# GpSimd waits by semaphore for the VectorE instructions at the shared SBUF port: attention and mixer on one core

## The chip, the cores and the metric

One core of a Trainium2 chip. The metric is device time in microseconds, the median of several runs. PE is TensorE, DVE VectorE, ACT ScalarE, POOL GpSimd, SP the engine that issues the transfers. DVE and POOL share a port to SBUF, the on-chip memory; the kernel's planner calls it `port`.

## The reference

Attention over 8 batches and 8 heads (sequence 576, head size 64) with a mask in blocks of 64, then a mixer over the sequence with a rank of 32 and a two-layer network, all in float32:

```python
scores = scale * np.matmul(q, k.transpose(0, 1, 3, 2))
scores = np.where(block_i >= block_j, scores, -1000000000.0)
attn = np.exp(scores - np.max(scores, axis=-1, keepdims=True))
attn = attn / (np.sum(attn, axis=-1, keepdims=True) + 1e-09)
x = np.matmul(attn, v)            # heads side by side: (8, 576, 512)
...
h = x.transpose(0, 2, 1) @ U @ V  # (576, 32), (32, 576)
u = x + h.transpose(0, 2, 1)
return u + np.maximum(u @ w_ch1, 0.0) @ w_ch2   # (512, 2048), (2048, 512)
```

## The kernel before, in words

**Precision.** A float32 operand goes through PE as a high part and a low part. ACT rounds the high part, and DVE or POOL subtracts it from the whole for the low part. So most products need three passes on PE, and each operand costs work on ACT and on DVE or POOL.

**Stages.** The program has two. Up to about 640 us the 64 heads run one after another: scores (L1224, L1228, L1229) into PSUM, row maxima on DVE (L1242), exponentials on ACT (L1253), the inverse of the row sums on DVE (L1269, L1270), the scaling of the probabilities `p` by it on POOL (L1279, five row tiles per head), transposes of `p` on PE (L1312), their halves on ACT and DVE (L1289, L1331), the product with v (L1371), the sum of its halves on DVE (L1379) and, after every second head, the mixing over the sequence (L1397 to L1444). From head 14 on, q and k are split too: ACT makes the high parts, POOL the low ones (L1170, L1171), and SP moves halves to the other partitions (L1173, L1174); POOL also makes the low half of v (L1193). Between these, PE works through the first part of the network (chunks of 288 tokens by 768 of the 2048 hidden columns: L651, L676), whose low halves of u POOL makes (L629, L635). The rest of the network, a block product in seven stages in the manner of Strassen (L897), fills the second part, from about 740 us to the end. Its sums and halves run on DVE and ACT (L822 to L858); POOL has nothing to do there.

**Weights.** They arrive as 64-bit words. `split64` (line 325) puts each piece together: ACT takes the absolute value of the upper word, POOL bounds it (L369), and DVE shifts it (L345), puts in the sign bit (L350) and the lower bits (L358). Low halves of scaled weights come from L466, those of batch 0's u from L620; for the block product POOL and DVE form sums and low halves 1280 columns wide (L753). `multiply` (L435) is a product of two columns, one number per partition.

**The order.** `Plan.add` (line 158) records each task with its engine, an assumed duration, a priority and what it reads and writes, and varies the duration by up to ±2% with a number drawn from `VARIANT`. `Plan.issue` (line 175) then walks through time: whenever an engine is free, it starts the ready task of the best priority, and the instructions are written down in that order, each engine's queue in its own. A task may be marked `port`; all POOL tasks count as marked. Line 201 doesn't start a marked task while another marked one runs:

```python
if all(b.pool for b in new) and not (port and tasks[n][7]):
    break
```

This shapes the order of the queues only. On the chip each engine goes through its queue on its own and waits by semaphore for the data that it needs, for nothing else. Marked on DVE are L345, L350, L358, L466, L620, L753, L824 and L834; not marked are `multiply` and the sums of the block product.

Of the kernel before, what the change touches and what calls it, by code (L numbers as in the profile page):

```python
# [27 lines left out]
T = 288  # L28
# [28 lines left out]

TAIL = {"PE": 165, "DVE": 78, "ACT": 105, "POOL": 20, "SP": 0}
INTO = {"PE": 355, "DVE": 60, "ACT": 60, "POOL": 200, "SP": 60}
NEAR, DL = 130, 3000  # L60
VARIANT = 11
START = {"DVE": 5750, "ACT": 2750, "POOL": 3300, "SP": 700}
COL = 0.4555
LA, MP = 900.0, 500.0
# [82 lines left out]
class Plan:  # L147
# [24 lines left out]
            b.users += 1  # L172
        self.tasks.append((engine, ns, prio, fn, deps, after, slots, port or engine == "POOL"))

    def issue(self):
        tasks = self.tasks
        users = [[] for _ in tasks]
        left = [len(t[4]) for t in tasks]
        for n, t in enumerate(tasks):
            for d in t[4]:  # L180
                users[d].append(n)
        others = [{tasks[u][0] for u in x} for x in users]
        ready = {e: [] for e in ENGINES}
        busy = dict.fromkeys(ready, False)
        port = False
        for n, t in enumerate(tasks):
            if not left[n]:
                heapq.heappush(ready[t[0]], (t[2], n))
        events, now, done = [], 0, 0
        for e, x in START.items():  # L190
            busy[e] = True
            heapq.heappush(events, (x, 0, -1, e))
        while done < len(tasks):
            for e, q in ready.items():
                if busy[e]:
                    continue
                later = []
                while q:
                    n = heapq.heappop(q)[1]
                    new = [b for b in tasks[n][6] if b.ap is None]  # L200
                    if all(b.pool for b in new) and not (port and tasks[n][7]):
                        break
                    later.append((tasks[n][2], n))
                    n = None
                else:
                    n = None
                for x in later:
                    heapq.heappush(q, x)
                if n is None:
                    continue  # L210
                for b in new:
                    b.ap = b.pool.pop(0)
                done += 1
                tasks[n][3]()
                busy[e] = True
                port = port or tasks[n][7]
                end = now + tasks[n][1]
                heapq.heappush(events, (end, 0, n))
                t = end + tasks[n][5] + TAIL[e]
                heapq.heappush(events, (t + 35, 1, n))  # L220
                for x in others[n]:
                    heapq.heappush(events, (t + INTO[x], 3 + ENGINES.index(x), n))
                if not tasks[n][5]:
                    heapq.heappush(events, (end + (0 if e == "PE" else NEAR), 2, n))
            now = events[0][0]
            while events and events[0][0] <= now:
                _, kind, n, *e = heapq.heappop(events)
                if e:
                    busy[e[0]] = False
                    continue  # L230
                if kind == 0:
                    busy[tasks[n][0]] = False
                    port = port and not tasks[n][7]
                    continue
                if kind == 1:
                    for b in tasks[n][6]:
                        b.users -= 1
                        if not b.users:
                            b.pool.append(b.ap)
                    continue  # L240
                for u in users[n]:

                    near = tasks[u][0] == tasks[n][0] and not tasks[n][5]
                    if kind == (2 if near else 3 + ENGINES.index(tasks[u][0])):
                        left[u] -= 1
                        if not left[u]:
                            heapq.heappush(ready[tasks[u][0]], (tasks[u][2], u))
# [6 lines left out]
def _dve(n):  # L254
    return 69 + 1.042 * n
# [13 lines left out]
def attention_then_mixer(  # L269
# [10 lines left out]
    nc = tc.nc  # L280
# [49 lines left out]
    def split64(fetches, shape, hi, lo, dst, prio, gate=(), part=slice(None), whole=None):  # L330

        n = 1
        for x in shape[1:]:
            n *= x
        rows = shape[0]
        st, zt = take(st_r, "st"), take(z_r, "z")
        s, z = st[:rows, :n, :], zt[:rows, :n]
        low, upp = s[:, :, 0], s[:, :, 1]

        def fetch():  # L340
            for f in fetches:
                f(s)

        def shift():
            nc.vector.tensor_scalar(  # L345
                out=z, in0=z, scalar1=3, scalar2=0x3FFFFFFF, op0=ALU.logical_shift_left, op1=ALU.bitwise_and
            )

        def put_upper():
            nc.vector.scalar_tensor_tensor(  # L350
                out=z, in0=upp, scalar=-(1 << 30), in1=z, op0=ALU.bitwise_and, op1=ALU.bitwise_or
            )

        def put_lower():
            o, l, x = z, low, z
            if whole:
                o, l, x = whole().bitcast(I32), *(a.rearrange("p (a b) -> p a b", a=2) for a in (low, z))
            nc.vector.scalar_tensor_tensor(  # L358
                out=o, in0=l, scalar=29, in1=x, op0=ALU.logical_shift_right, op1=ALU.bitwise_or
            )  # L360

        zf = f32(z)
        if len(shape) > 2:
            zf = zf.rearrange("p (a b) -> p a b", a=shape[1])
        add("SP", max(630 * len(fetches), 2.85 * n), prio, fetch, gate, [st], after=DL)
        add("ACT", _act(n, True) + (40 if n > 200 else 0), prio, lambda: nc.scalar.activation(f32(z), f32(upp), AF.Abs), [st], [zt])
        add(
            "POOL", 145 + 0.85 * n, prio,
            lambda: nc.gpsimd.tensor_scalar(out=f32(z), in0=f32(z), scalar1=MOST, scalar2=LEAST, op0=ALU.min, op1=ALU.max),  # L369
            [], [zt],  # L370
        )
        add("DVE", 50 + 0.55 * n, prio, shift, [st, zt], [zt], port=True)
        add("DVE", 13 + 1.15 * n, prio, put_upper, [st, zt], [zt], port=True)
        if whole:
            add("DVE", 100 + 1.15 * n, prio, put_lower, [st, zt], dst if isinstance(dst, list) else [dst], port=True)
            return
        add("DVE", 100 + 1.15 * n, prio, put_lower, [st, zt], [zt], port=True)
        add("ACT", _act(n, True), prio, lambda: nc.scalar.copy(hi(), zf), [zt], [dst])
        add("POOL", 60 + 2.3 * n, prio, lambda: nc.gpsimd.tensor_sub(lo(), zf[part], f32(hi()[part])), [zt, dst], [dst])
# [52 lines left out]
    def multiply(out, x, y, k, prio):  # L432
        add(
            "DVE", 70, prio,
            lambda: nc.vector.scalar_tensor_tensor(  # L435
                out=out.ap, in0=x[:, 1:2], scalar=k, in1=y.ap[:, -1:], op0=ALU.mult, op1=ALU.mult
            ),
            [x, y], [out],
        )

    banks_s = Part(banks_f, banks_f)
# [258 lines left out]
    def block_products():  # L700
# [146 lines left out]
                [x[1], iv, y[1]], [out[1]],  # L847
            )

        def vector(op, out, x, y, n=2):  # L850
            add("DVE", _dve(n * T), E, lambda: getattr(nc.vector, op)(out[0](), x[0](), y[0]()), [x[1], y[1]], [out[1]])

        def copied(out, x, iv=None, n=2):
            if iv is None:
# [6 lines left out]
        def blocks(src, stages, early=False, sc=None, wide=lambda j: 2):  # L861


            of = {}

            def total(out, x, y):
                for j, (o, a, b) in enumerate(zip(src[out], src[x], src[y])):
                    vector("tensor_sub", o, a, b, wide(j))

            for n, (_, x) in enumerate(stages):  # L870
                before = {y for _, y in stages[:n]}

                if x in ("t1", "t2") and not before & {"t1", "t2"}:
                    total("b11", "b12", "b11")
                if x == "t2":
                    at_t2 = "b11" if "t1" in before else "t2"
                    total(at_t2, "b22", "b11")
                if x == "t3":
                    if early:
                        of["b22"] = [piece(y, sc, wide(j)) for j, y in enumerate(src["b22"])]  # L880
                    total("b12", "b22", "b12")
                if x == "t4":
                    total("b21", "b21", at_t2)
                if x not in of:
                    at_x = {"t1": "b11", "t3": "b12", "t4": "b21"}.get(x, x) if x != "t2" else at_t2
                    of[x] = [piece(y, sc, wide(j)) for j, y in enumerate(src[at_x])]
                yield of[x]
# [611 lines left out]
    for c in range(CPB, NCHUNK):  # L1499
        ffn_chunk(c, lambda: wa, wab)  # L1500
    block_products()
    plan.issue()


# [36 lines left out]
```

## Time and profile before

| what | value |
| --- | --- |
| median of 3 runs | 1150.09 us (1149.17 to 1152.79) |
| the profiled execution | 1147.96 us |
| its span, first to last instruction | 1146.2 us |
| PE busy | 1117.5 us, 98% |
| DVE, ACT, POOL busy | 1010.0, 814.2, 516.2 us |
| granted PE clock | 0.999 |

The span is what the profile's instructions cover; the profiled execution's time is 1.8 us more. POOL's 516.2 us all lie before 714 us. A row of the timeline gives the start and the length in us; a group's row ends with its busy time and the mean length in ns, and then the idle time of the engine before it.

### The profile page before, as it was taken

The numbers are of one execution on the slowest core, as the hardware profiler recorded it, in microseconds if no ns is written. First come the engines' busy times: TensorE is split into PE (matmuls) and PEld (weight loads), VectorE is DVE, ScalarE is ACT, GpSimd is POOL, SyncE is SP. The second block draws the span as 40 slices with busy tenths as digits, with TensorE's granted clock in tenths as the row PEclk, the third lists the DMA queues.
The fourth block names the chain that finished last, engine by engine and source line by source line (L and its number), as shares of the span: only waits on it lengthen the run. The fifth ranks groups of instructions, "written<-read, shape, count | busy, mean of one in ns | idle before, by whom it ended". The sixth has DMA issues, their size and how long they took to land.

```text
span 1146.2 us, 25475 instructions
## 1 busy us (share of the span) xinstructions
PE 1117.5 (98%) x8952; PEld 928.8 (81%) x8952; DVE 1010.0 (88%) x2247; ACT 814.2 (71%) x1994; POOL 516.2 (45%) x688
## 2 busy tenths in 40 slices
PE   9999999999999899999998999999999999999998
PEld 7888888888888788888887877777777777777776
DVE  6899899999899898999898864399999899999998
ACT  7888998988998899998988744154545554454543
POOL 5444758787878777877876877000000000000000
PEclk9999999999999999999999999999999999999999
DMA  4443585364554546535442141204031231404111
GB/s 136 146 122 118 169 236 147 89 162 139 130 154 129 134 121 174 156 105 163 134 122 68 59 140 52 73 1 125 31 95 58 67 97 29 122 13 116 32 53 43
DMA packets 76720, 122.14 MB, mean 107 GB/s; under 512 B 9008, under 2 KB 53040, under 8 KB 76592
## 3 DMA queue, kind: packets, MB, share of 16 engines
q1 hardware_dynamic: 76592, 120.51, 36.9%
q8 instruction: 71, 1.16, 0.5%
q14 instruction: 57, 0.47, 0.1%
HBM read 76.23 MB, written 29.49 MB: 92 GB/s over the span
## 4 chain that ended last, share of the span: by engine, by line
PE 67%; DVE 17%; ACT 9%; issue 3%; DMA 2%; POOL 1%; SPq 0%; ACTq 0%; POOLq 0%; DVEq 0%
PE bb L897 36%; PE bf L651 7%; PE bf L676 7%; PE ba L1312 5%; ACT p L1253 4%; DVE mx L1242 4%; PE ba L1371 3%; DVE pl L1331 3%; PE ba L1355 2%; ACT ph L1289 1%; PE ba L1397 1%; DVE xt L1379 1%; PE ba L1228 1%; DVE hl L659 1%; PE bw L1228 1%
## 5 line engine op out<-in xcount | busy, mean ns | idle before, releaser
L1279 POOL TENSOR_SCALAR p<-p,rv 128x576 f32<-128x576 f32 (+4 forms) x320 | 174.6, 559 | 94.1 <-DVE rv L1270 55.9
L897 PE MATMUL bb<-ph,w2h 128*128 128x288 f16 x560 | 151.0, 286 | 0.0
L897 PE MATMUL bb<-ph,w2l 128*128 128x288 f16 x560 | 151.0, 286 | 0.0
L897 PE MATMUL bb<-ph,w1h 128*128 128x288 f16 x560 | 148.7, 286 | 0.0
L897 PE MATMUL bb<-ph,w1l 128*128 128x288 f16 x560 | 148.7, 286 | 0.0
L822 ACT CAST ph<-hb 128x576 f16<-128x576 f32 x144 | 84.3, 590 | 82.8 <-PE bb L897 77.2
L897 PEld LDWEIGHTS <-w1h 128*128 128x128 f16 x1120 | 109.6, 98 | 27.6
L897 PEld LDWEIGHTS <-w2h 128*128 128x128 f16 x1120 | 109.6, 98 | 27.6
L1312 PE MATMUL ba<-ident,p 128*128 128x128 f32 x768 | 122.2, 275 | 3.5 <-DVE xt L1379 2.1
L897 PE MATMUL bb<-pl,w2h 128*128 128x288 f16 x560 | 123.6, 286 | 0.0
L897 PE MATMUL bb<-pl,w1h 128*128 128x288 f16 x560 | 114.4, 286 | 0.0
L1331 DVE TENSOR_TENSOR pl<-ba,ph 128x512 fp32r<-128x512 f32 x200 | 106.4, 551 | 8.7 <-ACT ph L1289 5.6
L676 PE MATMUL bf<-hh,w2h 128*128 128x288 f16 x384 | 110.4, 288 | 0.0
L676 PE MATMUL bf<-hl,w2h 128*128 128x288 f16 x384 | 109.8, 286 | 0.0
L676 PE MATMUL bf<-hh,w2l 128*128 128x288 f16 x384 | 109.8, 286 | 0.0
L1289 ACT CAST ph<-ba 128x512 fp32r<-128x512 f32 x200 | 93.1, 494 | 7.8 <-PE ba L1312 5.6
L1312 PEld LDWEIGHTS ba<-ident,p 128*128 128x128 f32 x768 | 90.5, 142 | 8.3 <-POOL vs L1193 2.1
L824 DVE TENSOR_TENSOR pl<-hb,ph 128x576 f16<-128x576 f32 x144 | 91.4, 653 | 1.0
L1253 ACT ACTIVATE p<-ba,mx 64x64 f32<-64x64 f32 (+1 forms) x176 | 85.6, 491 | 7.6 <-DVE mx L1242 6.6
L676 PEld LDWEIGHTS <-w2h 128*128 128x128 f16 x768 | 75.2, 98 | 19.0 <-issue 0.7
L651 PEld LDWEIGHTS <-w1h 128*128 128x128 f16 x768 | 72.8, 98 | 21.8 <-issue 4.0
L1371 PE MATMUL ba<-ph,vs 128*128 128x256 f32 (+3 forms) x400 | 85.9, 271 | 1.6 <-DVE ut L1432 1.2
(191 smaller groups left out, 3136.7 us busy)
## 6 DMA issues: line engine op xcount, KB each, us to landing
raw<-in_qk_dram SPq DMA_DIRECT2D x63, 288.0 KB, 3.9
o_d<-ot SPq DMA_DIRECT2D x72, 144.0 KB, 2.2
vr<-in_v_dram SPq DMA_DIRECT2D x32, 320.0 KB, 3.8
ur<-u_d SPq DMA_DIRECT2D x64, 144.0 KB, 2.6
wr<-o_d SPq DMA_DIRECT2D x32, 288.0 KB, 3.0
out_dram<-wr SPq DMA_DIRECT2D x31, 288.0 KB, 2.3
st<-in_w_dram SPq DMA_DIRECT2D x16, 512.0 KB, 4.1
u_d<-ut SPq DMA_DIRECT2D x28, 288.0 KB, 2.2
```

Source lines behind the costliest of these rows:

```text
L651: nc.tensor.matmul(ps[:, :T], w()[wn][:, k, fs], m[k].ap, start=(i == 0), stop=(i == len(ops) - 1))
L676: nc.tensor.matmul(ps[:, :T], w()[wn][:, f, ms], hs[f][x].ap, start=(i == 0), stop=(i == len(ops) - 1))
L822: add("ACT", _act(n * T, True), E, lambda: nc.scalar.copy(h.ap[:, :n, :], x[0]()), [x[1]], [h])
L824: "DVE", _dve(n * T), E, lambda: nc.vector.tensor_sub(l.ap[:, :n, :], x[0](), h.ap[:, :n, :]), [x[1], h], [l],
L897: nc.tensor.matmul(bank[:, i, :T], x()[:, w(k)], p.ap[:, k, :], start=first and n == 0, stop=last and n == len(ops) - 1)
L1242: lambda i=i, at=at: nc.vector.tensor_reduce(out=mx[: P if i else 64, i : i + 1], in_=view(i, at), op=ALU.max, axis=AX.XY if i == 4 else AX.X,
L1253: nc.scalar.activation(out.rearrange("p (j k) -> p j k", j=2) if i == 4 else out, view(i, at), AF.Exp, bias=mx[:rows, i : i + 1], accum_ou ...
L1279: lambda x=x, rows=rows, i=i: nc.gpsimd.tensor_scalar(out=x, in0=x, scalar1=rv[:rows, i : i + 1], scalar2=1.0, op0=ALU.mult, op1=ALU.mult),
L1289: add("ACT", _act(n), pr, lambda: nc.scalar.copy(out(), inp()), reads, writes)
L1312: nc.tensor.transpose(out=bank[:, a : a + P], in_=pt_r[i][h % PB[i]][:, j * P : (j + 1) * P], identity=perm.ap)
L1331: "DVE", _dve(m), pr, lambda: nc.vector.tensor_sub(pl[:, low], bank[:, :m], f32(ph[:, low])), [bank, bh], [bl]
L1371: nc.tensor.matmul(bank[0 : c.stop, a:n], vs[:, j, c], x[:, _at(g, j)], start=(i == 0), stop=(i == len(ops) - 1))
```

## The change

The planner gets three additions and a new number for `VARIANT`.

- Behind each marked DVE task, POOL is held in the plan until `PORT` = 200 ns after its planned end.
- The first POOL instruction that is written down after a marked DVE instruction gets a dependency with a semaphore on the last such DVE instruction. As each engine keeps its order, all POOL instructions behind it wait as well. A DVE instruction doesn't wait for POOL.
- `multiply` (L435) and the subtractions (`total`) ahead of the block product (part of L851) are marked `port` too.
- `VARIANT` goes from 11 to 4: every assumed duration is varied by another draw, so the order is planned anew.

The functions of marked tasks now return their instruction (`return` in `shift`, `put_upper`, `put_lower`). The diff, without those lines:

```diff
-NEAR, DL = 130, 3000
-VARIANT = 11
+NEAR, DL, PORT = 130, 3000, 200
+VARIANT = 4
...
-        port = False
+        port, held, last = False, 0, None
+        behind = mybir.DependencyInfo(mybir.DependencyClass.Sync, mybir.DependencyReason.DATA)
...
-                    if all(b.pool for b in new) and not (port and tasks[n][7]):
+                    if all(b.pool for b in new) and not (port and tasks[n][7]) and not (e == "POOL" and now < held):
                         break
...
-                tasks[n][3]()
+                x = tasks[n][3]()
+                if e == "POOL" and last is not None:
+                    tc.add_manual_dep(x.ins, last.ins.name, behind, reason="port")
+                    last = None
+                if e == "DVE" and tasks[n][7]:
+                    last = x
+                    held = now + tasks[n][1] + PORT
+                    heapq.heappush(events, (held, -1, n))
...
                 if e:
                     busy[e[0]] = False
+                    continue
+                if kind == -1:
                     continue
...
@@ multiply
-            [x, y], [out],
+            [x, y], [out], port=True,
...
-        def vector(op, out, x, y, n=2):
-            add("DVE", _dve(n * T), E, lambda: getattr(nc.vector, op)(out[0](), x[0](), y[0]()), [x[1], y[1]], [out[1]])
+        def vector(op, out, x, y, n=2, port=False):
+            add(
+                "DVE", _dve(n * T), E, lambda: getattr(nc.vector, op)(out[0](), x[0](), y[0]()), [x[1], y[1]], [out[1]],
+                port=port,
+            )
...
-                    vector("tensor_sub", o, a, b, wide(j))
+                    vector("tensor_sub", o, a, b, wide(j), True)
```

More of the change, by code (lines that the diff above doesn't have):

```diff
@@ L173, in add, with issue @@
         self.tasks.append((engine, ns, prio, fn, deps, after, slots, port or engine == "POOL"))
-    def issue(self):
+    def issue(self, tc):
         tasks = self.tasks
@@ L344, in shift @@
         def shift():
-            nc.vector.tensor_scalar(
+            return nc.vector.tensor_scalar(
                 out=z, in0=z, scalar1=3, scalar2=0x3FFFFFFF, op0=ALU.logical_shift_left, op1=ALU.bitwise_and
@@ L349, in put_upper @@
         def put_upper():
-            nc.vector.scalar_tensor_tensor(
+            return nc.vector.scalar_tensor_tensor(
                 out=z, in0=upp, scalar=-(1 << 30), in1=z, op0=ALU.bitwise_and, op1=ALU.bitwise_or
@@ L357, in put_lower @@
                 o, l, x = whole().bitcast(I32), *(a.rearrange("p (a b) -> p a b", a=2) for a in (low, z))
-            nc.vector.scalar_tensor_tensor(
+            return nc.vector.scalar_tensor_tensor(
                 out=o, in0=l, scalar=29, in1=x, op0=ALU.logical_shift_right, op1=ALU.bitwise_or
@@ L1501, in attention_then_mixer @@
     block_products()
-    plan.issue()
+    plan.issue(tc)
 def _layout(inputs):
```

## The prediction

> **What bounds the kernel now.** I read the head of the page first.
>
> ```profile
> span 1146.2 us, 25475 instructions
> PE 1117.5 (98%) x8952; PEld 928.8 (81%) x8952; DVE 1010.0 (88%) x2247; ACT 814.2 (71%) x1994; POOL 516.2 (45%) x688
> ```
>
> TensorE is busy for 1117.5 of 1146.2 us. No edit that leaves its matmuls alone can win more than the idle 28.7 us, so the question is where those lie. The table by stretches (columns: length, then busy time of PE, PEld, DVE, ACT and POOL, each with its count of instructions) answers it.
>
> ```profile
> 0.00:180.00 180.00, 173.61 (x1175) 146.25 (x1176) 158.40 (x458) 155.53 (x427) 96.68 (x155) 1.00 0.52 153
> 180.00:640.00 460.00, 442.88 (x3689) 382.66 (x3688) 420.89 (x1101) 413.95 (x1148) 358.56 (x489) 1.00 0.47 131
> 640.00:740.00 100.00, 98.27 (x806) 78.45 (x805) 56.32 (x94) 43.46 (x81) 60.98 (x46) 1.00 0.30 90
> 740.00:1100.00 360.00, 360.00 (x2941) 287.55 (x2940) 335.08 (x532) 182.50 (x308) 0.00 (x0) 1.00 0.23 67
> ```
>
> From 740 to 1100 us PE never rests and POOL does nothing: that stage stays as it is. Before 740 PE idles 740 − (173.61 + 442.88 + 98.27) = 25.2 us, two thirds of it (17.1) between 180 and 640. There PE, DVE and ACT are all busy over 90% and POOL 78%: four engines in lockstep, with PE taking its work in a fixed order, so that whatever holds DVE for 2 us holds PE soon after.
>
> Then I looked at what holds DVE: the timeline of DVE, POOL and PE around the longest gap of PE (start us, length, engine, line, operation, out<-in; in brackets idle time before it and who ended it).
>
> ```profile
> 611.38 3.64 DVE L435 SCALAR_TENSOR_TENSOR iv<-sc 128x1 f32<-128x1 f32 x1
> 615.05 0.16 DVE L435 SCALAR_TENSOR_TENSOR iv<-sc,iv 128x1 f32<-128x1 f32 x1
> ...
> 611.41 0.86 POOL L1193 TENSOR_TENSOR vs<-vr,vs 128x320 fp32r<-128x320 f32 x1
> 612.26 1.36 POOL L1279 TENSOR_SCALAR p<-p,rv 128x576 f32<-128x576 f32 x2
> ...
> 614.07 1.25 POOL L1279 TENSOR_SCALAR p<-p,rv 128x320 f32<-128x320 f32 x3
> ...
> 615.87 0.30 PE L1397 MATMUL ba<-ident,xt 128*64 128x128 f32 x1 [2.94 <-DVE xl L1403]
> ```
>
> One product of two columns on DVE, 0.16 us when it runs alone, lasts 3.64 us, and all the while POOL starts one instruction after another. DVE's next instructions come 3.5 us late and PE stands 2.94 us. The rule in line 201 never plans a POOL instruction beside a DVE instruction marked `port`, but nothing on the chip keeps it, and this line 435 isn't marked at all. The same picture stands at six more places; first the stalled DVE instruction of each, then PE's idle time behind it.
>
> ```profile
> 157.19 1.54 DVE L345 TENSOR_SCALAR z<-z 128x320 int32<-128x320 int32 x1
> ...
> 213.30 2.37 DVE L345 TENSOR_SCALAR z<-z 128x320 int32<-128x320 int32 x1
> ...
> 256.00 1.60 DVE L358 SCALAR_TENSOR_TENSOR wr<-st,z 128x320 int32<-128x320 int32 x1
> ...
> 396.05 2.61 DVE L350 SCALAR_TENSOR_TENSOR z<-st,z 128x320 int32<-128x320 int32 x1
> ...
> 476.31 1.90 DVE L358 SCALAR_TENSOR_TENSOR spare<-st,z 128x512 int32<-128x512 int32 x1
> ...
> 680.10 2.47 DVE L851 TENSOR_TENSOR z<-hb,u 128x576 f32<-128x576 f32 x1
> ```
>
> ```profile
> 159.15 0.65 PE L651 MATMUL bf<-uh,w1h 128*128 128x288 f16 x4 [1.24 <-DVE hl L659]
> ...
> 216.15 0.52 PE L1312 MATMUL ba<-ident,p 128*128 128x128 f32 x3 [1.91 <-DVE xt L1379]
> ...
> 258.39 0.47 PE L1371 MATMUL ba<-ph,vs 128*128 128x256 f32 x2 [0.97 <-DVE ut L1432]
> ...
> 399.32 0.40 PE L1427 MATMUL ba<-v,t 96*128 96x288 f32 x1 [2.71 <-DVE pl L1331]
> ...
> 478.60 0.33 PE L1312 MATMUL ba<-swap,p 128*128 128x128 f32 x1 [1.01 <-DVE xt L1379]
> ...
> 683.00 0.65 PE L651 MATMUL bf<-uh,w1h 128*128 128x288 f16 x4 [1.12 <-DVE hl L659]
> ```
>
> The seven gaps of PE add up to 2.94 + 1.24 + 1.91 + 0.97 + 2.71 + 1.01 + 1.12 = 11.9 us, almost half of the 25.2. The chain of waits that ended last runs through the stalled instructions themselves, so no hidden third party ends those gaps:
>
> ```profile
> 213.38 2.29 DVE z L345
> ...
> 611.38 3.65 DVE iv L435
> ```
>
> **The change, part by part.** *What the stalls are worth.* Unstalled lengths, from the groups of a quiet stretch (144 to 148 us) and from the groups of the whole run:
>
> ```profile
> L350 DVE SCALAR_TENSOR_TENSOR z<-st,z 128x320 int32<-128x320 int32 x2 | 0.9, 476 | 0.0
> L345 DVE TENSOR_SCALAR z<-z 128x320 int32<-128x320 int32 x2 | 0.5, 310 | 0.0
> L358 DVE SCALAR_TENSOR_TENSOR wr<-st,z 128x320 int32<-128x320 int32 x1 | 0.5, 474 | 0.0
> ```
>
> ```profile
> L358 DVE SCALAR_TENSOR_TENSOR wr<-st,z 128x512 int32<-128x512 int32 x6 | 4.1, 680 | 0.1
> L851 DVE TENSOR_TENSOR z<-ur,ur 128x576 f32<-128x576 f32 x7 | 5.3, 751 | 0.0
> ```
>
> The excess at the seven places is 1.54 − 0.31 = 1.23, 2.37 − 0.31 = 2.06, 1.60 − 0.47 = 1.13, 2.61 − 0.48 = 2.13, 1.90 − 0.68 = 1.22, 3.64 − 0.16 = 3.48 and 2.47 − 0.75 = 1.72. PE regains at each place the smaller of the excess and its gap: 1.23 + 1.91 + 0.97 + 2.13 + 1.01 + 2.94 + 1.12 = **11.3 us**. With the new wait a POOL instruction that stands behind the DVE one in the order can't start before it has ended, and then the long stalls can't happen: they need POOL to run ahead. What may remain is a stall on a POOL instruction that stands in front, for the rest of that one. I take the order to be the running-ahead kind, because at 611 us at least five POOL instructions start while DVE waits. Lines 435 and 851 join only because the diff now marks them; without those marks the term would be 7.3.
>
> The Trainium skill (SBUF — State Buffer, section Who interferes with whom) says that the one of the two that starts first has the shared pair for its whole instruction and the other blocks until it has finished. The trace has DVE waiting through several in a row, so blocking agrees and "until the first finishes" doesn't; its consequence is the second rival.
>
> *The price on POOL.* Each marked DVE instruction now gets one wait on POOL. What is queued behind it is all of POOL's later work: the scaling of `p` (L1279), which PE's transposes (L1312) need, and the low halves of q and k (L1170, L1171), which SP's transfers (L1173) and PE's scores need. How long a hand-over lasts, the trace shows for another pair: `rv` ends at 205.17 and POOL starts at 205.27.
>
> ```profile
> 204.99 0.18 DVE L1270 RECIPROCAL rv<-rv 128x3 f32<-128x3 f32 x1
> ...
> 205.27 0.93 POOL L1279 TENSOR_SCALAR p<-p,rv 128x320 f32<-128x320 f32 x2 [1.17 <-DVE rv L1270]
> ```
>
> So 0.1 us beside the length of the DVE instruction: about 0.5 + 0.1 = 0.6 us of POOL's time per wait. Between 180 and 640 us the marked instructions are, with their busy time and count:
>
> ```profile
> 180.00:640.00 460.00, 12.70 (x22) 1.00 0.47 131
> ...
> 180.00:640.00 460.00, 17.56 (x22) 1.00 0.47 131
> ...
> 180.00:640.00 460.00, 16.54 (x22) 1.00 0.47 131
> ...
> 180.00:640.00 460.00, 7.17 (x14) 1.00 0.47 131
> ```
>
> That is L345, L350, L358 and L435, 80 in all. 80 x 0.6 = 48 us go into POOL's idle 460 − 358.6 = 101.4 us: that is the cover, and POOL climbs from 78% to about 88% occupied. PE's own waits for POOL are small today:
>
> ```profile
> PE ba L1312 <- POOL p L1279: 1.2, 2, 1.0
> ```
>
> A POOL with half its slack gone makes PE wait oftener. From below, nothing (the delayed POOL work had slack); from above, one more such wait of up to 1.0 us at each of the seven places, 7 us. I take **2.5 us**, nearer to the low end, because the row shows only 2 waits in 1146 us. Were the cover gone, all of it beyond 101.4 us would fall on the path; that is the first rival.
>
> *The planner.* It holds POOL for 200 ns behind each marked instruction and draws its ±2% with another number, so the order of everything changes. Nothing in the trace prices that; it can help or hurt. The idle time of PE that isn't behind the seven stalls is 25.2 − 11.9 = 13.3 us; a new order deals it anew. I take 0 and, as an estimate, a third of it, 4 us, to either side.
>
> *The marks on the subtractions of the last stage* cost nothing after 740 us (POOL 0.00). From 640 to 740 the planner may place them later, behind POOL's long L753; PE's 98.27 of 100 us of matmuls there hide it, and without that cover the stage would lose up to POOL's 60.98 us.
>
> Sum: 11.3 − 2.5 = 8.8 us less. Against the profiled execution (1147.96 us, span 1146.2 and 1.8 around it) 1139.2; that execution is 2.1 us below the median of the runs, so against 1150.09 the forecast is **1141.3 us**.
>
> **The rivals.** *POOL becomes the bound (slower).* If DVE comes late to its marked instructions, POOL waits not 0.6 us but DVE's whole lag. It decides from 101.4 / 80 = 1.27 us per wait. At 1.5 us, POOL overruns the stage by 120 − 101.4 = 18.6 us, less the 11.3 regained: +7.3, 1157.4. For it: POOL at 78% in a stage whose other engines are above 90%. Against it: DVE is the faster for each stall that goes. Chance 0.11.
>
> *A smaller gain.* A GpSimd instruction that stands in front in the order still blocks, or only one instruction's worth of each stall was the port's. The long POOL instruction of that stage is L1171:
>
> ```profile
> L1171 POOL TENSOR_TENSOR k<-raw,k 64x576 fp32r<-64x576 f32 x50 | 72.4, 1449 | 11.0 <-ACT k L1169 10.8
> ```
>
> A cap of 1.45 us per place makes the term 1.23 + 1.45 + 0.97 + 1.45 + 1.01 + 1.45 + 1.12 = 8.7, the gain 8.7 − 2.5 = 6.2, the time 1143.9; with the order term against it, 1148. Chance 0.20. This is the time that the rule of the Trainium skill's page SBUF — State Buffer, told above, would lead to.
>
> *Nothing moves.* The stalls go, but PE then waits at the same places for POOL's late `p` and `k` (7 us) and the order term takes the rest, 4; or the wait doesn't bite, because the POOL instructions involved stand in front. 1150. Chance 0.14.
>
> **How the numbers follow.** Forecast 0.55, smaller gain 0.20, nothing 0.14, slower 0.11. A measurement of this kernel can tell about 0.3% (3.5 us) from no change: faster 0.75, same 0.14, slower 0.11. Low end: all 11.3 and the order term, 1150.1 − 15.3 = 1134.8; high end: the no-change case with half the order term against it, 1152. About 0.08 lies beyond each.
>
> **What would show it.** Right: L345, L350, L358 and L435 keep within 0.2 us of their unstalled lengths; POOL's waits name these lines, some 80 times or fewer after 180 us, mostly under 1 us; PE's idle time before 740 us falls from 25 to about 16; PE waits for POOL 3 to 4 us in all; the last stage keeps its length. Wrong: DVE stalls of over 1.5 us that remain (the smaller gain), POOL above 90% busy with waits of over 1.3 us (the slower case), or PE's idle time unchanged with POOL's or ACT's name on it.

## The result, and the profile after

The changed kernel takes **1132.32 us** (median of 4 runs, 1131.96 to 1132.71), the kernel before, beside it, 1149.63 us (1147.52 to 1152.79): ratio **0.9847**, 95% interval 0.9824 to 0.9871. That is 17.3 us less, where 8.8 were forecast. The way was right, the size was about half.

The head of the page after:

```profile
span 1130.7 us, 25478 instructions
PE 1114.4 (99%) x8952; PEld 929.1 (82%) x8952; DVE 992.4 (88%) x2247; ACT 809.8 (72%) x1994; POOL 495.0 (44%) x688
```

Of the 15.5 us between the two spans 12.4 are idle time of PE (28.7 to 16.3), and 3.1 are busy time of PE for the same 8952 matmuls. DVE's and POOL's busy time fell by 17.6 and 21.2 us for the same instructions: an instruction that stalls counts as busy, so the stalls at the port are in those times. The table by stretches (length, busy time of PE, PEld, DVE, ACT and POOL, granted clock, DMA):

```profile
0.00:180.00 180.00, 173.84 (x1154) 144.92 (x1155) 156.17 (x450) 153.47 (x425) 89.61 (x151) 1.00 0.52 147
180.00:640.00 460.00, 453.70 (x3827) 395.80 (x3826) 414.31 (x1123) 417.34 (x1163) 360.38 (x503) 1.00 0.49 135
640.00:740.00 100.00, 99.59 (x816) 79.25 (x815) 60.32 (x99) 43.73 (x78) 45.01 (x36) 1.00 0.27 81
740.00:1100.00 360.00, 360.00 (x2941) 287.54 (x2940) 335.55 (x534) 182.62 (x308) 0.00 (x0) 1.00 0.23 67
```

PE idles 740 − (173.84 + 453.70 + 99.59) = 12.9 us before 740 us, where it idled 25.2. Nearly all of the difference lies between 180 and 640 us (17.1 to 6.3), where the stalls were. The last stage is the same.

The marked DVE instructions (the line, its count, min / median / max in ns; L355, L360, L368 and L445 are the lines 345, 350, 358 and 435 of before):

```profile
L355 DVE TENSOR_SCALAR z<-z x44: 169/358/654, 8.9 to 607.6; 128x512 int32<-128x512 int32 x16, 128x320 int32<-128x320 int32 x16, 128x384 int32<-128x384 int32 x8, 96x288 int32<-96x288 int32 x2
```

```profile
L360 DVE SCALAR_TENSOR_TENSOR z<-st,z x44: 187/554/1154, 9.1 to 608.3; 128x512 int32<-128x512 int32 x16, 128x320 int32<-128x320 int32 x16, 128x384 int32<-128x384 int32 x8, 96x288 int32<-96x288 int32 x2
```

```profile
L445 DVE SCALAR_TENSOR_TENSOR iv<-sc,iv x17: 140/149/725, 99.6 to 661.5; 128x1 f32<-128x1 f32 x17
L445 DVE SCALAR_TENSOR_TENSOR iv<-sc x3: 139/155/199, 81.0 to 632.2; 128x1 f32<-128x1 f32 x3
```

The longest shift fell from 2.37 to 0.65 us, the longest L360 from 2.61 to 1.15, and the product of two columns that had lasted 3.64 us takes 0.20. What is left I read as the rest of a POOL instruction that stands ahead in the order. Around that product the timeline of DVE and then POOL now reads:

```profile
632.23 0.20 DVE L445 SCALAR_TENSOR_TENSOR iv<-sc 128x1 f32<-128x1 f32 x1
632.46 0.86 DVE L445 SCALAR_TENSOR_TENSOR iv<-sc,iv 128x1 f32<-128x1 f32 x7
...
632.50 0.45 POOL L1431 TENSOR_TENSOR t<-tz,t 32x128 fp32r<-32x128 f32 x1
633.49 0.31 POOL L1292 TENSOR_SCALAR p<-p,rv 64x64 f32<-64x64 f32 x1 [0.54 <-DVE iv L445]
```

L1431 still runs beside the products; then POOL stands 0.54 us for them. POOL's waits in sum (us, times, longest):

```profile
POOL p L1292 <- DVE rv L1283: 18.3, 16, 3.3
...
POOL p L1292 <- DVE wr L368: 12.1, 5, 4.4
...
POOL p L1292 <- DVE z L360: 4.7, 5, 1.8
...
POOL p L1292 <- DVE z L355: 3.3, 5, 0.9
...
POOL p L1292 <- DVE iv L445: 2.9, 3, 1.8
```

POOL waits for the marked lines, once for 4.4 us, but its wait for `rv`, 55.9 us on the page of before, shrank to 18.3: much of the time that it now stands for a marked instruction it used to stand for the inverse. PE's waits show who pays:

```profile
PE ba L1325 <- POOL p L1292: 1.7, 3, 1.3
...
PE ba L1325 <- DVE xt L1392: 1.2, 4, 0.5
...
PE bf L661 <- DVE hl L669: 0.9, 2, 0.4
```

But for the start of the program no wait of PE for DVE is over 0.5 us, where 2.9 was the longest; for POOL's `p` PE waits 1.7 us instead of 1.2.

### The profile page after: what moved, and what is told of

It reads as the page before. It is cut to its first block, busy times and chain, and to the rows that moved or that the text cites. A ratio compares the mean times of both kernels' runs of the same rounds, so it can differ in the third digit from the quotient of the medians.

```text
span 1130.7 us, 25478 instructions
## 1 busy us (share of the span) xinstructions
PE 1114.4 (99%) x8952; PEld 929.1 (82%) x8952; DVE 992.4 (88%) x2247; ACT 809.8 (72%) x1994; POOL 495.0 (44%) x688
## 4 chain that ended last, share of the span: by engine, by line
PE 67%; DVE 16%; ACT 10%; issue 3%; DMA 2%; POOL 1%; SPq 0%; ACTq 0%; DVEq 0%; POOLq 0%
PE bb L910 36%; PE bf L686 8%; PE bf L661 6%; PE ba L1325 5%; ACT p L1266 4%; DVE mx L1255 4%; DVE pl L1344 3%; PE ba L1384 3%; PE ba L1368 2%; ACT ph L1302 1%; DVE xt L1392 1%; PE bw L1237 1%; DMA raw<-in_qk_dram 1%; DVE hl L669 1%; DVE ut L1445 1%
## 5 line engine op out<-in xcount | busy, mean ns | idle before, releaser
L1292 POOL TENSOR_SCALAR p<-p,rv 128x576 f32<-128x576 f32 (+4 forms) x320 | 166.2, 533 | 88.1 <-DVE rv L1283 18.3
```

Source lines behind the costliest of these rows:

```text
L1292: lambda x=x, rows=rows, i=i: nc.gpsimd.tensor_scalar(out=x, in0=x, scalar1=rv[:rows, i : i + 1], scalar2=1.0, op0=ALU.mult, op1=ALU.mult),
```

## The experiments

Three theories stood against each other. A: the stalls are worth nearly all of it, in more ways than the seven gaps. B: the stalls are worth the 8.8 us, and the new order of the instructions brought the rest. C: the new order brought everything. Each ratio is against runs of the kernel before on the same chip.

**1. The wait alone, in the order of before** (`e1_wait_only`). The planner is left as it was; a mark of its own says where POOL waits.

```diff
-        self.tasks.append((..., port or engine == "POOL"))
+        self.tasks.append((..., port or engine == "POOL", port or mark))
...
+                if e == "POOL" and last is not None:
+                    tc.add_manual_dep(x.ins, last.ins.name, behind, reason="port")
+                    last = None
+                if e == "DVE" and tasks[n][8]:
+                    last = x
```

Expected: 

> The order of the kernel before, unchanged (VARIANT 11, no hold of 200 ns, no new marks in the planner); only the semaphore of POOL on the marked DVE instructions is added, the ones that the change marks newly (L435, part of L851) among them. Theory A (the stalls of DVE at the port, the small ones too, are worth nearly the whole gain, and the waits on POOL cost next to nothing): 0.985 to 0.990 of before, 1133 to 1139 us. Theory B (the stalls are worth the 8.8 us that was forecast, the rest of the 17 us is the new order): 0.991 to 0.994, 1140 to 1143 us. Theory C (the new order is everything, waits on POOL eat what the stalls give): 0.997 to 1.003.

Measured: 1137.29 us, ratio 0.9881 (0.9858 to 0.9905), 13.9 us less than the 1151.23 beside it. Theory A's range. PE's busy time in the middle stage rises from 442.88 to 452.84 us:

```profile
180.00:640.00 460.00, 452.84 (x3794) 392.06 (x3794) 419.84 (x1119) 422.61 (x1165) 360.42 (x496) 1.00 0.47 132
```

Of the 11.9 us in PE's seven gaps 2.9 are left (counting what is over 0.3 us): 0.55 at the first place, 0.51 at the one of 396 us, and 1.85 at the last, where it was 1.12. The subtraction that stalled there takes 0.92 us now, but the next one meets the POOL instruction that is already running:

```profile
668.36 3.12 POOL L759 TENSOR_TENSOR w2l<-spare,w2h 128x1280 f16<-128x1280 f32 x1
...
669.29 2.80 DVE L857 TENSOR_TENSOR hb<-hb 128x576 f32<-128x576 f32 x1
...
673.91 0.65 PE L657 MATMUL bf<-uh,w1h 128*128 128x288 f16 x4 [1.85 <-DVE hl L665]
```

**2. The plan alone** (`e2_plan_only`): the changed kernel without the line `tc.add_manual_dep(...)`.

Expected: 

> The changed kernel without the semaphore: its order stays as it is (VARIANT 4, POOL held for 200 ns in the plan, new marks), only the waits on the chip go. Theory A: stalls of DVE over 1 us come back, 0.995 to 1.002 of before. Theory B: the new order alone gives about half of the gain, 0.991 to 0.994. Theory C: as fast as the changed kernel, 0.984 to 0.987.

Measured: 1147.7 us, 0.9976 (0.9955 to 0.9997). The stalls are back, in places of their own; one product of two columns lasts 3.66 us and one shift 2.68:

```profile
L444 DVE SCALAR_TENSOR_TENSOR iv<-sc,iv x17: 140/153/3661, 100.4 to 674.8; 128x1 f32<-128x1 f32 x17
```

```profile
L354 DVE TENSOR_SCALAR z<-z x44: 184/356/2683, 8.8 to 621.3; 128x512 int32<-128x512 int32 x16, 128x320 int32<-128x320 int32 x16, 128x384 int32<-128x384 int32 x8, 96x288 int32<-96x288 int32 x2
```

So holding POOL in the plan doesn't hold it on the chip. Only the semaphore does.

**3. and 4. The draw** (`e3_before_v4`: `VARIANT = 4` in the kernel before; `e4_after_v11`: `VARIANT = 11` in the changed one).

Expected of the first: 

> The kernel before with VARIANT 4 in place of 11 and nothing else: another draw of the assumed durations, so another order. Theory A: within 0.997 to 1.005 of before. Theories B and C: 0.990 to 0.995, if the number itself is what is good in the new order; above 0.997, if the hold or the marks are.

Expected of the second: 

> The changed kernel with VARIANT 11, the number of the kernel before: semaphore, hold and marks as in the change. Theory A: 0.984 to 0.990 of before, since the draw doesn't matter. Theory B with the draw as the good part: 0.990 to 0.994. Theory C with the draw as the good part: 0.997 to 1.003.

Measured: 1147.73 us, 0.9964 (0.9947 to 0.9982), and 1137.21 us, 0.9882 (0.9858 to 0.9906). The changed kernel with the old draw is as fast as the wait alone (1137.29): the hold of 200 ns and the new marks in the planner bring nothing in sum. The first ratio lies just below theory A's range; every execution of that kernel ran at a mean clock of 1.000, and at full clock the kernel before takes 1147.59 (one execution, see 5), so without the wait the draw is worth nothing. From draw 11 to draw 4, with the wait, the time falls from 1137.21 to 1132.32: 4.9 us, from two comparisons. Their ratios carry the clock of before, and the intervals overlap (0.9858 to 0.9906, 0.9824 to 0.9871); but both kernels ran at 0.999 or 1.000, and the fastest execution with draw 11, 1136.44, lies well above the slowest with draw 4, 1132.71. Of the 5.4 us between the two traces' spans 1.6 are idle time of PE and 3.8 its busy time for the same matmuls (1118.2 to 1114.4; the profile models when a matmul ends, so this is rough). Theory B holds for these 4.9 us, and for these alone.

**5. The old marks only** (`e5_old_marks`): as 1, without waits behind `multiply` and the subtractions of the block product.

Expected: 

> As e1_wait_only, but POOL waits only for the DVE instructions that the kernel before marks; L435 and the subtractions of L851 stall as before. Theory A (every gap of PE behind a long stall counts one for one): the gaps of 2.94 and 1.12 us come back, about 4 us above e1_wait_only: 0.991 to 0.993 of before. Rival (something else is next late at these two places): within 0.2% of e1_wait_only, 0.987 to 0.990.

Measured: 1145.12 us, 0.9946 (0.9925 to 0.9967). Half of the gain of 1 is gone, 7.8 us and not 4: above both expected ranges. The timeline shows the stall of 3.64 us and PE's gap of 2.94 behind it, as before:

```profile
611.16 3.64 DVE L441 SCALAR_TENSOR_TENSOR iv<-sc 128x1 f32<-128x1 f32 x1
...
615.64 0.30 PE L1403 MATMUL ba<-ident,xt 128*64 128x128 f32 x1 [2.94 <-DVE xl L1409]
```

and the table by stretches shows what comes behind the gap (the third number from the end is the granted clock):

```profile
612.00:615.00 3.00, 0.70 (x6) 0.32 (x4) 2.97 (x3) 1.02 (x1) 3.00 (x7) 1.00 0.00 0
616.00:619.00 3.00, 3.00 (x16) 2.19 (x14) 2.88 (x13) 2.91 (x9) 0.46 (x1) 0.51 0.14 46
```

PE, set free, runs at half clock for 3 us and does 16 matmuls. The same stall in the kernel before had no such tail in its profiled execution, but the gap at 396 us had. Here are the stretches with these two gaps and those behind them, cut at the steps of 3.41 us at which the clock can change (see the last section):

```profile
396.44:399.85 3.41, 0.70 (x6) 0.43 (x5) 3.41 (x4) 3.00 (x8) 2.77 (x5) 1.00 0.00 0
399.85:403.26 3.41, 3.41 (x18) 2.63 (x16) 3.05 (x8) 1.36 (x3) 1.08 (x1) 0.50 0.43 132
403.26:406.67 3.41, 3.41 (x33) 3.30 (x32) 2.66 (x7) 2.55 (x6) 1.43 (x1) 1.00 0.39 84
...
611.48:614.89 3.41, 1.44 (x13) 1.02 (x11) 3.41 (x1) 1.77 (x3) 3.41 (x6) 1.00 0.00 0
614.89:618.30 3.41, 2.43 (x25) 2.17 (x25) 3.31 (x13) 2.10 (x7) 1.79 (x3) 1.00 0.00 0
```

The stretch at half clock holds 18 matmuls, the next one at full clock 33. So a gap of PE of 2 to 3 us may cost 1.7 us (half of 3.4, an estimate) more than it lasts. The executions of the kernel before carry this in their mean clock: on the chip of experiment 1, the one at 1.000 took 1147.59 us, the seven at 0.997 took 1148.4 to 1151.2, the five at 0.994 took 1153.8 to 1158.4. All runs of experiment 1 are at 0.999 or 1.000 and lie within 1.0 us. What stood ahead of the stretches at half clock in the executions without a profile isn't on record.

Not all of the 7.8 us is the port's. This profiled execution is the slowest of the eight; of its four windows of 3.4 us at half clock three stand behind gaps of PE at 477.8 and 530.8 us, just ahead of which ACT waits 3.48 and 3.69 us for transfers. And of the two places left unguarded only that of L435 stalled as before: the subtraction of the seventh took 0.74 us, and the next one 2.81, with a gap of 1.69 us behind it, much as in experiment 1.

**6. and 7. The seven places, alone and left out** (`e6_seven_only`, `e7_all_but_seven`), in the order of before:

```diff
-                if e == "DVE" and tasks[n][8]:
+                if e == "DVE" and n in SEVEN:                          # 6
+                if e == "DVE" and tasks[n][8] and n not in SEVEN:      # 7
```

Expected of 6: 

> The order of the kernel before, with the semaphore at the seven places alone that the prediction lists. If its term of 11.3 us was right and its price of 2.5 us was not: 0.989 to 0.991 of before. If the seven are worth only about half of that, and the rest comes from the many small stalls: 0.993 to 0.997. If stalls only move on to the next marked instruction: above 0.997.

Expected of 7: 

> The other half of e6_seven_only: the semaphore at all marked DVE instructions but those seven. If the seven are worth 11.3 of the 14 us: 0.996 to 1.000 of before. If the small stalls are worth about half: 0.992 to 0.995. If waits on POOL have a price of several us that the gains of e1_wait_only hide: above 1.000.

Measured: 1142.14 us, 0.9916 (0.9891 to 0.994), and 1136.94 us, 0.9871 (0.985 to 0.9891), against 1151.82 on their chip. The seven alone bring 9.7 us, the others without the seven 14.9, as much as all together. The two don't add up, and none of my expectations for either held (6 lies between two of its ranges). At full clock the seven alone bring less, 6.9 us: 1146.76 to 1139.83, one execution each. In the trace of 6 all seven instructions have their unstalled lengths (0.31, 0.31, 0.49, 0.47, 0.68, 0.16 and 0.74 us), so at each place the POOL instruction in the way stood behind in the order. The profile of 7 says why it gains as much: the shifts and the products at the seven places are stalled little or not at all there although nothing guards them.

```profile
L352 DVE TENSOR_SCALAR z<-z x44: 169/378/1236, 9.2 to 570.2; 128x512 int32<-128x512 int32 x16, 128x320 int32<-128x320 int32 x16, 128x384 int32<-128x384 int32 x8, 96x288 int32<-96x288 int32 x2
```

```profile
L442 DVE SCALAR_TENSOR_TENSOR iv<-sc,iv x17: 146/151/721, 102.0 to 657.8; 128x1 f32<-128x1 f32 x17
L442 DVE SCALAR_TENSOR_TENSOR iv<-sc x3: 129/155/160, 76.9 to 602.7; 128x1 f32<-128x1 f32 x3
```

The longest shift is 1.24 us instead of 2.37, the column product 0.16 instead of 3.64. One of the seven stays, the L358 of 1.60 us:

```profile
L365 DVE SCALAR_TENSOR_TENSOR wr<-st,z x30: 460/542/1604, 29.9 to 400.7; 128x320 int32<-128x320 int32 x16, 128x384 int32<-128x384 int32 x8, 128x512 int32<-128x512 int32 x6
```

My reading is that the stalls are linked: a wait anywhere brings POOL back in step with DVE, so it isn't ahead at the next marked instruction either. The two runs show that the places aren't independent; the link itself was not tried by itself.

**8. The price of a wait** (`e8_wait_all_dve`): as 1, but POOL waits for the last DVE instruction of any kind (a few, such as the inverse of the row sums, return no instruction and set no wait).

```diff
-                if e == "DVE" and tasks[n][8]:
+                if e == "DVE" and x is not None:
```

Expected: 

> As e1_wait_only, but POOL waits for the last DVE instruction of any kind ahead of it in the order, marked or not: many times the waits, none of which frees the port. Theory that POOL's waits cost next to nothing, since the order is planned in step: within 0.3% of e1_wait_only, 0.986 to 0.992 of before. Theory that each wait has a price which PE sees (2.5 us for some 80 waits in the prediction): 0.993 or more, above before if POOL becomes the bound.

Measured: 1156.76 us, 1.0041 (1.0028 to 1.0055): slower than before, 19.5 us above experiment 1. PE's wait for POOL's `p` is 13.9 us here, against 2.1 in 1, and it is the first of PE's waits:

```profile
PE ba L1318 <- POOL p L1285: 13.9, 20, 1.8
```

So waits have a price, and the slower rival's mechanism exists: too many waits make POOL late for PE. POOL's queue in the trace waits on DVE's semaphore 134 times before, 192 times in 1 and 577 times here: 19.5 us for 385 more waits, 0.05 us each. At that rate the 58 waits that 1 adds would cost 2.9 us, an estimate, close to the 2.5 of the prediction; what the trace of 1 shows is 0.9 us more of PE's wait for `p` (1.2 to 2.1).

**9. and 10. Two more draws** (`e9_after_v2`, `e10_after_v7`: the changed kernel with `VARIANT` 2 and 7).

Expected of the first: 

> The changed kernel with VARIANT 2: another order, semaphore, hold and marks kept. Theory (the draw is worth some 4 us either way, and 4 is a good one): 0.985 to 0.995 of before, above the changed kernel's 0.985. Rival (the order of the changed kernel is better for a reason other than the draw): within 0.2% of the changed kernel.

Expected of the second: 

> As e9_after_v2 with VARIANT 7. Theory: 0.985 to 0.995 of before, and a few us apart from e9_after_v2. Rival: within 0.2% of the changed kernel.

Measured: 1140.14 us, 0.9887 (0.9855 to 0.9918), and 1137.11 us, 0.9867 (0.9832 to 0.9903). With draws 11 (1137.21) and 4 (1132.32) four orders span 8 us, and 4 is the best of them by about 5. What in that order is better stays open.

**11. Both ways** (`e11_both_ways`): in the changed kernel a marked DVE instruction also waits for the last POOL instruction ahead of it.

```diff
+                if e == "POOL":
+                    ahead = x
                 if e == "DVE" and tasks[n][7]:
+                    if ahead is not None:
+                        tc.add_manual_dep(x.ins, ahead.ins.name, behind, reason="port")
+                        ahead = None
                     last = x
```

Expected: 

> The changed kernel with the opposite semaphore as well: a marked DVE instruction also waits for the last POOL instruction ahead of it in the order. It takes away what is left of POOL stalled by DVE, about nothing on PE's path. Theory (the gain lies in DVE not being overtaken; DVE is the busier engine, and its waits cost): 0 to 1% slower than the changed kernel, 0.985 to 0.995 of before. Rival (every overlap at the port costs): faster than the changed kernel, 0.980 to 0.984.

Measured: 1136.05 us, 0.9849 (0.9822 to 0.9877). No faster than the changed kernel: by its median 3.7 us slower, as the theory has it. The ratios are alike, but before ran mostly at 0.994 to 0.997 beside this one, and both changed kernels at 0.999 or 1.000, so I go by the medians.

**12. The seven delays without the port** (`e12_seven_late`): experiment 1 with DVE held up by clearing a scratch tile at the seven places.

```diff
+                for at in range(0, int(960 * LATE.get(n, 0)), 448):
+                    m = min(448, int(960 * LATE[n]) - at)
+                    tc.nc.vector.memset(self.scratch[:, :m], 0.0)
                 x = tasks[n][3]()
```

Expected: 

> e1_wait_only with artificial delays: ahead of each of the seven DVE instructions that the prediction lists, DVE clears a scratch tile for as long as the stall took (1.23, 2.06, 1.13, 2.13, 1.22, 3.48 and 1.72 us by the counting of one column per cycle; what a clearing takes the trace shows). No port is involved. Theory 1 (a stall costs PE what it lasts): 9 to 12 us above e1_wait_only, 0.996 to 0.999 of before, clock 1.000. Theory 2 (a gap of PE of 2 to 3 us also brings stretches of half clock, which are part of the cost): above theory 1 by 2 to 4 us and clocks of 0.995 to 0.999 in most executions, 0.998 to 1.003 of before. Theory 3 (the seven are only the sign of POOL running ahead, and DVE has slack for them): less than 5 us above e1_wait_only, below 0.993.

Measured: 1153.2 us, 1.0003 (0.9985 to 1.002), mean clocks of 0.992 to 0.997: the whole gain of experiment 1 is gone, as theory 2 has it, with clocks still lower than it expected. The clearings took longer than the stalls they stand for: they step by 0.59 us each, so at the longest place DVE is held from 616.58 to 620.90, 4.3 us, and over all seven 15.7 instead of 13.0. By the medians, on two chips, that gives back 15.9 us. Clearing and PE's gap there, and PE at a bit over half clock behind it (0.57 over the stretch):

```profile
616.58 0.43 DVE L218 MEMSET scratch<- 128x448 f32 x1
...
620.13 0.77 DVE L218 MEMSET scratch<- 128x448 f32 x2 [0.16 <-DVE scratch L218]
```

```profile
621.76 0.30 PE L1408 MATMUL ba<-ident,xt 128*64 128x128 f32 x1 [3.63 <-DVE xl L1414]
```

```profile
617.00:622.00 5.00, 1.37 (x12) 0.94 (x11) 3.90 (x12) 1.46 (x2) 0.72 (x1) 1.00 0.00 0
...
623.00:627.00 4.00, 4.00 (x27) 3.17 (x25) 2.87 (x11) 3.97 (x9) 3.68 (x6) 0.57 0.34 109
```

Between the profiled executions of 12 and 1 lie 21.0 us. PE idles 14.0 us more, 12.0 of them at the seven places (14.9 against 2.9), and is busy 6.9 us longer for the same matmuls (1122.9 against 1116.0), with five windows of half clock in the trace. So a late DVE at these places costs PE less than it lasts in gaps, 12.0 of 15.7 us, and the clock comes on top, whoever makes it late. POOL is held with DVE here, as it waits for the same instructions; PE's wait for `p` is 2.5 us, so this adds little.

## Why the prediction was wrong in size

The mechanism was right: stalls of DVE at the port hold PE, and the semaphore removes them (experiments 1 and 2). The sum failed in two of its steps, the clock behind a gap and the draw. Its middle part came out near the measured net, in part because errors cancel.

- **"PE regains at each place the smaller of the excess and its gap: 11.3 us", less 2.5.** At full clock before takes 1147.59 us on the chip of experiment 1 (one execution) and the wait alone 1137.29: 10.3 us, against 8.8. But the seven gaps gave back 9.0 us and not 11.3, mainly since the stall at the last place moved on to the next subtraction; POOL's price shows as 0.9 us and not 2.5; and the rest came from places that the sum doesn't list. That the net is near is partly luck.
- **The same step, what it left out.** It priced a gap of PE at its length. A gap of 2 to 3 us is often followed by 3.4 us at half clock, 1.7 us more. I had the profiled execution, with one such stretch. Each takes about 0.0015 off the mean clock (1.7 of 1146 us, an estimate), so the executions of before at 0.997 to 0.994 have two to four, and the changed kernel has none. That is how I read what lies between 1147.6 and the medians: 2.0 us in the comparison of the result, 3.6 in that of experiment 1.
- **"The planner … I take 0."** The draw was worth 4.9 us (experiments 3 and 4), more than the 4 that I had allowed, and only with the wait. The 4 was a third of PE's remaining idle time, but between the two traces 3.8 of 5.4 us are PE's busy time for the same matmuls. So the idle time, which the prediction takes at its start as the most that can be won, isn't a strict bound. Why the matmuls take less in that order stays open. The hold of 200 ns that I had named with it was worth nothing.
- 10.3 + 2.0 + 4.9 = 17.2 of the 17.3 us. This sum closes by construction, as its terms are the steps from 1149.63 to 1147.59, to 1137.29 and to 1132.32; it doesn't prove the split. My low end, with 11.3 + 4, left out the clock and set the draw too small, and so 1132.3 lies below 1134.8.
- **The price on POOL** was of the right kind (experiment 8) and mostly hidden: PE waits 1.7 us for `p` instead of 1.2. The wait added 58 waits to POOL's queue in experiment 1, where I had counted 80 in the middle stage alone. **POOL becomes the bound** needs several times as many waits.
- **"Without those marks the term would be 7.3"**, less the same 2.5, is a net of 4.8. Experiment 5 kept 6.7 us, but its times hold late transfers and half clock, so it doesn't test the size.
- **"The same picture stands at six more places"** is true of two of them. At 213 and 396 us POOL starts another instruction while DVE waits, as at 611. At 157, 256 and 680 us one POOL instruction, already running, is in the way, and at 476 DVE gets in after the first of two. The rows of POOL at 213, 476 and 680 us:

```profile
213.25 1.41 POOL L1171 TENSOR_TENSOR k<-raw,k 64x576 fp32r<-64x576 f32 x1
214.63 0.85 POOL L1193 TENSOR_TENSOR vs<-vr,vs 128x320 fp32r<-128x320 f32 x1
...
476.26 1.41 POOL L1171 TENSOR_TENSOR k<-raw,k 64x576 fp32r<-64x576 f32 x1
477.63 1.86 POOL L1170 TENSOR_TENSOR q<-raw,q 64x576 fp32r<-64x576 f32 x1
...
679.35 2.61 POOL L753 TENSOR_TENSOR w2l<-spare,w2h 128x1280 f16<-128x1280 f32 x1
```

- **The smaller gain** rested on a cap of one POOL instruction per stall, as the Trainium skill (SBUF — State Buffer, Who interferes with whom) has it. Four of the seven places agree with that rule. The stall of 3.64 us, which comes again in experiment 5, lasts through at least five POOL instructions: here the measurement differs from the page. But what decided against this rival is the order: all seven instructions lose their stalls in experiment 6, so none of the POOL instructions stood in front.
- **Of the signs** two came out otherwise. The longest L360 is still 1.15 us, more than 0.2 us above its unstalled length, and PE's idle time before 740 us fell to 12.9 us, not 16.

## What to carry to other kernels

Where two engines share a port, a plan that keeps their instructions apart holds only as long as the engines keep its pace; a semaphore that lets the less loaded engine wait for the busier one was worth far more here than better planning, as long as it stood only where the port is really contended. Price a gap of TensorE at its length and the half clock that may follow it, and look at the clocks of many executions, not of the profiled one alone. And before a change that redraws an order is credited with a gain, run the old draw with the new rule.

## What the runs showed of the hardware

A DVE instruction of 0.16 us lasted 3.64 us while POOL instructions followed each other without a pause, and those of 2.37 and 2.61 us too waited through more than one. It isn't always so: at 476 us DVE ended 0.54 us after the first of two POOL instructions, and the second took 1.86 us, where L1170 takes 1.42 in the mean.

Pauses of TensorE of 1.9 to 3.6 us were followed by half clock in some cases and not in others: 2.71 us at 396 in before was, 2.94 at 612 wasn't. The record of the clock in the traces tells what decides. In all fourteen, the changes of the clock lie whole multiples of 3.413 us apart, so there are fixed windows of that length, and a gap may fall into one window or be split by two. In the rows of before, PE idles 2.71 of the 3.41 us in the window at 396.44, and the next window has half clock; the longer gap at 612 is split, 1.97 us in the window at 611.48 and 0.98 in the next, and the clock stays. Between 20 and 1120 us the fourteen traces have eight windows with 2.06 us or more of idle PE, and half clock followed all eight; of eight with 1.77 to 1.97 us it followed three, and of those at full clock with less, none. So about half a window's idle time is the limit here, and it is the place of a gap against the windows that looks like chance.

The Trainium skill (TensorE: Matmul & The Clock Gate, section What's actually happening) tells of a free-running window of 3413 ns and of half clock after at least one idle window. The traces agree with the window and its length; a window that was idle for 1.8 to 3.0 us of it was enough here.
